# A gated-memory attention with two mixture layers: new numbers for the planner, q of block 0 turned from another queue, the router's fold in strips, a bound and a rounding on ScalarE

## The chip, the cores and the metric

The kernel runs on one core of a Trainium2 chip. The core has five engines with a queue each: TensorE (PE in the profile, PEld for its weight loads), VectorE (DVE), ScalarE (ACT), GpSimd (POOL) and SyncE (SP), which here only issues DMAs. Each works its queue in order. The metric is the time of one execution in microseconds; the median of three runs is given, lower is better.

## The reference, cut to what matters

```python
# attention: complex decay a per head and channel, only the real part of the state is read
scale = np.minimum(mag, 0.999) / (mag + 1e-06)          # mag = |a|
for t in range(S):                                      # S = 768, B = 4, H = 8, D = 48
    S_re, S_im = ar*S_re - ai*S_im + k[t] v[t]^T, ar*S_im + ai*S_re
    y[t] = q[t] @ S_re
x = (x @ w_a) * (x @ w_b) @ w_out                       # 3072 tokens, 384 -> 1536 -> 384
logits = x @ w_gate                                     # 8 experts
expert_idx = np.argmax(logits, axis=1)
out[mask] = gate_w[mask, None] * (np.maximum(x[mask] @ w1[e], 0.0) @ w2[e])
```

The attention is computed in chunks of 128 tokens. With the decay's logarithm summed along a chunk, q and k are multiplied by the magnitude (A or its inverse Bt) and by cosine and sine of the phase, and a masked product of both gives the same y. w_a, w_b and w_out arrive as 64-bit floats.

## The kernel before

There are 12 blocks of 256 tokens (two chunks each). For each block j the program has these parts:

- `loads` and `load_v` fetch re, im, q, k and v. `pre` computes on ACT, DVE and POOL the decay (`decay`, a scan), the tangent, the phase (`phase`, a scan), rounds the phase with MAGIC, takes cosine and sine, multiplies (`mul`) and turns the products with small DMAs into `kT` and `qT` (`turn`). For block 0 it is done in two halves of 128 tokens, which makes 12 turns for k and 12 for q, of 64 KB each.
- `attn` is the attention: scores `sc_p` (PE), `mask` to `sm` (DVE), k turned back `kn_p` (PE, copied by ACT), `y_p` (PE), then x as high and low part (`xH` on ACT, `xL` on DVE), and the state `kv_p` (PE), `T` (DVE).
- `planned_moe` is the first mixture: for each of 12 slices f, `up` writes `ab_p` (18 matmuls), ACT copies a half of it to g, DVE multiplies (`gate_b`), ACT makes gH, DVE or POOL gL, and `down` adds six products to `o`. Block 0 does it in plain fp32 with weights that were just unpacked (`up32`, `down32`, called the first gated products below); the later blocks do it with weights split into wH and wL (`parted`).
- `conv` loads one of 36 pieces of weights and unpacks it with three operations on DVE (L783, L786, L789: shift, low, sign). For each slice of w_out, PE also turns it (`wt_p`) and multiplies it with the router's weights (`wg_p`, the fold), with ACT copies between.
- Then the last block, and eight experts in a hand-merged order, from about 560 us on; the change doesn't touch this part.

Which engine's instruction stands where is not written by hand for the first 11 blocks. Each step is given to `Plan.add` with a cost, with what it reads and writes, and with a due time `at`; `Plan.run` simulates the five queues with these costs, takes the earliest step that is ready (on a tie that with the smaller due time), and then writes the instructions in that order. The chip follows this order on each queue, but not its times. PRE, ATT, CONV, M0, M1, SPLIT, SLOT, LOAD and AHEAD are the due times and paces; ON_POOL, GL_POOL and L_POOL say what goes to POOL instead of DVE. All the queues' DMAs stand on SP, except POOL's indirect ones.

Of the kernel before, what the change touches and what calls it, by code (L numbers as in the profile page):

```python
# [24 lines left out]
AHEAD = 14  # L25
LOAD = (4.0,2.0,7,30.0,2.0)
# [3 lines left out]
PRE = ((0.0, 20.0), (2.0, 22.0), (40.0, 70.0), (100.0, 125.0), (140.0, 166.0))  # L30
ATT = (26,66,110,156)
CONV = (22,1.8)
M0 = (40.0, 90.0)
M1 = 88
SPLIT = (84,1.2)
SLOT = 49.0
# [373 lines left out]
def fast(tc, q, k, v, a_re, a_im, w_a, w_b, w_out, w_gate, w1, w2, out, dram, x2d):  # L410

    nc = tc.nc
# [3 lines left out]
    with ExitStack() as mctx, ExitStack() as ctx:  # L416
# [18 lines left out]
        biases = const.tile([128, 4], F32, name="biases")  # L435
# [70 lines left out]
        def spans(i, src, nm, f, at):  # L506
# [13 lines left out]
            P.add("SP", 0.06, load, w=[("s", "bo"[i % 2], NF)], at=at, size=393, early=at)  # L520
# [235 lines left out]
        A32 = {}  # L756

        def conv(i, f, src, nm, at):
# [33 lines left out]
            P.add("SP", 0.06, load, r=[("bits", i - AHEAD)], w=[slot], at=start, early=start, size=393)  # L792
# [24 lines left out]
            t = P.add("PE", 0.28, turned, r=[slot], w=[("wt_p", f)], at=at + 2, take="sc")  # L817
            P.add("ACT", on("ACT", 384, True), kept, r=[("wt_p", f)], w=["rx"], at=at + 2, give=t)
            t = P.add("PE", 0.25, folded, r=["rx"], w=[("wg_p", f)], at=at + 3, take="sc")
# [115 lines left out]
        def planned_moe(j, lo, hi):  # L935
# [3 lines left out]
            def falls(f, at):  # L939
# [6 lines left out]
                for c in range(2):  # L946
                    P.add("ACT" if c == 0 else "DVE", on("DVE", DM) + 0.16, lambda c=c: close(j, c), r=[f"o{c}"] + ([("lgt", j % 2, 0)] if c else []), w=[("x2", c), ("lgt", j % 2, c)], at=at, alone=False)
                    P.add("SP", 0.06, lambda c=c: store(j, c), r=[("x2", c)], at=at, size=196)
# [30 lines left out]
        def load_v(j, c, at):  # L979
# [3 lines left out]
            P.add("SP", 0.06, go, w=[("v", (2 * j + c) % 3)], at=at, size=196)  # L983

        def loads(j, nms, at, parts=1):
# [17 lines left out]
            for i in range(2):  # L1003
                for nm in nms:
                    if parts == 1 and nm != "q":
                        if i == 0:
                            P.add("SP", 0.06, go(nm, 0, 2, True), w=[(nm, 0), (nm, 1)], at=at, size=393)
                    else:
                        made[nm, i] = \
                        P.add("SP", 0.06, go(nm, i, 1, i == 0), w=[(nm, 0), (nm, 1)] if i == 0 else [(nm, 1)], at=at + (4 if parts == 2 and i else 0), size=196, soft=made.get((nm, 0)))  # L1010

        def pre(j, lo, hi, t0, t1):
# [118 lines left out]
            add("DVE", lambda: nc.vector.tensor_scalar(out=T("Cc"), in0=T("F"), scalar1=MAGIC, scalar2=MAGIC, op0=ALU.add, op1=ALU.subtract), ks("F"), ks("Cc"), fast=True)  # L1131
            tt("frac", "F", "F", "Cc", ALU.subtract)
            add("DVE", lambda: nc.vector.tensor_copy(out=carry, in_=T("F")[:, :, n - 1, C - 1]), ks("F"), ["carry"], weight=0.16)
# [3 lines left out]
            act("F", "F", ACTF.Sin, scale=-TWO_PI)  # L1137

            def mul(src, c2, w):
                t = src if c2 else "Bt" if src == "k" else "A"  # L1140
                e, eng = pick(src + "01"[c2])

# [22 lines left out]
                for jj in range(3):  # L1165
                    first = c2 == 0 and lo == 0 and jj == 0
                    add("SP", turn(jj), ks(t) + [("column", t, lo)] + ([] if first else ks(src + "T")), (every(src + "T") if first else []) + [(src + "T", c, c2, jj) for c in cs], size=65 * n, key=src if first else None, soft=src)
# [5 lines left out]
            for i, (e, f, r, w, kw) in enumerate(todo):  # L1173
# [4 lines left out]
                if e == "SP":  # L1178
                    weight = 0.06
# [279 lines left out]
```

## Time and profile before

| | us |
|---|---|
| median of 3 runs (lowest, highest) | 935.42 (935.24, 936.86) |
| the profiled execution's own time | 934.75 |
| its span in the trace | 932.9 |
| PE busy | 865.6 (93%) |
| DVE busy | 606.7 (65%) |
| ACT busy | 446.6 (48%) |
| POOL busy | 288.5 (31%) |

The span runs from the first to the last instruction; 1.9 us lie around it. Busy shares are means over stages that differ: PE stands still for most of the first 41 us and is busy without a break for long stretches after. A busy PE is not PE at its peak.

### The profile page before, as it was taken

Reading aid. Unit: us, or ns where it says so; the run is one execution under the profiler, and the core shown is the slowest. Engines: PE = TensorE matmul, PEld = TensorE weight load, DVE = VectorE, ACT = ScalarE, POOL = GpSimd, SP = SyncE. Lnnn points to the kernel's source line nnn. Section 1 sums busy time; section 2 is a strip of 40 time slices with the busy share of each in tenths; the row PEclk is TensorE's granted clock in tenths of the full one; section 3 lists DMA queues with packets and bytes.
Section 4 is the critical chain, followed back from the end, with each engine's and each line's share of the span. In section 5 each row is a group of like instructions: output and inputs, shape, how many; then the busy total and the mean of one; then the engine's idle time right before and its main releaser. Section 6 shows DMA issues by size and latency. Waiting matters only on the chain. (4 is left out here: it accounts for less than half of the span.)

```text
span 932.9 us, 20023 instructions
## 1 busy us (share of the span) xinstructions
PE 865.6 (93%) x7948; PEld 829.9 (89%) x7948; DVE 606.7 (65%) x1261; ACT 446.6 (48%) x821; POOL 288.5 (31%) x285
## 2 busy tenths in 40 slices
PE   0399899899999999999999999999998999999993
PEld 0287789899999999999999999999997999999993
DVE  7799999968668678695858595325731644545440
ACT  6453567666656463645555552224531534434430
POOL 3100011143343334343434241213244451333311
PEclk9999999999999999999999999999998999999997
DMA  9394522540524643628172615024341543454601
GB/s 250 97 344 128 179 61 55 142 120 26 163 66 140 132 124 92 182 66 208 34 204 68 189 28 169 3 69 124 115 137 48 161 147 109 143 164 127 171 25 24
DMA packets 128900, 112.77 MB, mean 121 GB/s; under 512 B 36564, under 2 KB 123446, under 8 KB 128796
## 3 DMA queue, kind: packets, MB, share of 16 engines
q1 hardware_dynamic: 122620, 101.30, 38.0%
q0 software_dynamic: 6176, 10.08, 3.7%
q8 instruction: 65, 1.06, 0.5%
q14 instruction: 39, 0.32, 0.1%
HBM read 82.42 MB, written 10.56 MB: 100 GB/s over the span
## 5 line engine op out<-in xcount | busy, mean ns | idle before, releaser
L852 PE MATMUL ab_p<-xH,wa 128*128 128x256 f32 x792 | 168.4, 289 | 0.7 <-ACT xH L1259 0.7
L852 PE MATMUL ab_p<-xH,wb 128*128 128x256 f32 x792 | 162.6, 282 | 0.0
L880 POOL TENSOR_TENSOR gL<-g,gH 128x256 fp32r<-128x256 f32 x108 | 94.7, 877 | 213.0 <-ACT gH L876 204.9
L869 ACT COPY g<-ab_p 128x256 f32<-128x256 f32 x144 | 53.4, 371 | 181.8 <-PE ab_p L852 160.0
L889 PE MATMUL o<-wo,gH 128*128 128x392 f32 x528 | 139.7, 345 | 0.0
L852 PEld LDWEIGHTS ab_p<-xH,wa 128*128 128x128 f32 x792 | 131.3, 189 | 3.7 <-issue 1.9
L852 PEld LDWEIGHTS ab_p<-xH,wb 128*128 128x128 f32 x792 | 131.7, 190 | 0.0
L872 DVE TENSOR_TENSOR g<-g,ab_p 128x256 f32<-128x256 f32 x144 | 59.8, 415 | 99.8 <-ACT g L869 97.8
L852 PE MATMUL ab_p<-xL,wa 128*128 128x256 f32 x396 | 111.5, 282 | 1.8 <-DVE xL L1262 1.8
L852 PE MATMUL ab_p<-xL,wb 128*128 128x256 f32 x396 | 111.6, 282 | 0.0
L715 DVE SCALAR_TENSOR_TENSOR hL<-h_p,hH 128x256 fp32r<-128x256 f32 (+5 forms) x80 | 41.3, 517 | 97.2 <-ACT hH L714 85.5
L714 ACT ACTIVATE hH<-h_p 128x256 fp32r<-128x256 f32 (+5 forms) x80 | 36.6, 459 | 119.4 <-PE h_p L710 102.4
L889 PE MATMUL o<-wo,gL 128*128 128x392 f32 x264 | 90.1, 341 | 0.0
L889 PEld LDWEIGHTS o<-wo,gH 128*128 128x128 f32 x528 | 89.1, 189 | 0.7 <-issue 0.6
L710 PE MATMUL h_p<-sH,w1H 128*128 128x256 f32 (+5 forms) x240 | 78.3, 326 | 4.3 <-issue 4.0
L728 PE MATMUL o<-w2H,hH 128*128 128x384 f32 (+4 forms) x232 | 79.8, 344 | 0.0
L728 PE MATMUL o<-w2H,hL 128*128 128x384 f32 (+4 forms) x232 | 79.0, 341 | 0.0
L728 PE MATMUL o<-w2L,hH 128*128 128x384 f32 (+4 forms) x232 | 78.9, 340 | 0.0
L710 PE MATMUL h_p<-sH,w1L 128*128 128x256 f32 (+5 forms) x240 | 77.4, 323 | 0.0
L710 PE MATMUL h_p<-sL,w1H 128*128 128x256 f32 (+5 forms) x240 | 77.3, 322 | 0.0
L852 PEld LDWEIGHTS ab_p<-xL,wa 128*128 128x128 f32 x396 | 75.1, 190 | 2.4 <-DVE xL L1262 2.2
L876 ACT ACTIVATE gH<-g 128x256 fp32r<-128x256 f32 x132 | 54.6, 414 | 46.1 <-DVE g L872 45.2
(193 smaller groups left out, 1920.4 us busy)
## 6 DMA issues: line engine op xcount, KB each, us to landing
raw<-in_moe_w_dram SPq DMA_DIRECT2D x64, 384.0 KB
q<-in_q_dram SPq DMA_DIRECT2D x24, 192.0 KB
v<-in_v_dram SPq DMA_DIRECT2D x24, 192.0 KB
raw<-in_moe_w_a_dram SPq DMA_DIRECT2D x12, 384.0 KB
raw<-in_moe_w_b_dram SPq DMA_DIRECT2D x12, 384.0 KB
raw<-in_moe_w_out_dram SPq DMA_DIRECT2D x12, 384.0 KB
x2d<-x SPq DMA_DIRECT2D x24, 192.0 KB
ck<-in_moe_w_a_dram SPq DMA_DIRECT2D x12, 384.0 KB
```

The costliest lines, as they stand in the source:

```text
L710: nc.tensor.matmul(out=t, lhsT=lh[:, o:o + 128], rhs=rh[:, kk].rearrange("p c t -> p (c t)"), start=n == 0, stop=n == 8)
L714: nc.scalar.activation(out=hH, in_=t, func=ACTF.Relu)
L715: nc.vector.scalar_tensor_tensor(out=hL, in0=t, scalar=0.0, in1=hH.bitcast(F32), op0=ALU.max, op1=ALU.subtract)
L728: nc.tensor.matmul(out=G["o", c], lhsT=lh[:, c * r:(c + 1) * r], rhs=rh, start=f == 0 and n == 0, stop=f == NH - 1 and n == 2)
L852: nc.tensor.matmul(out=t[:, i], lhsT=lh[:, kk * 128:(kk + 1) * 128], rhs=rh[:, kk], start=n == 0, stop=n == 8)
L869: nc.scalar.copy(out=G["g", j, f], in_=G["ab", j, f][:, 0])
L872: nc.vector.tensor_tensor(out=G["g", j, f], in0=G["g", j, f], in1=G["ab", j, f][:, 1], op=ALU.mult)
L876: nc.scalar.activation(out=G["H", j, f], in_=G["g", j, f], func=ACTF.Copy)
L880: eng.tensor_tensor(out=G["L", j, f], in0=G["g", j, f], in1=G["H", j, f].bitcast(F32), op=ALU.subtract)
L889: nc.tensor.matmul(out=G["o", j, c], lhsT=lh[:, c * C:(c + 1) * C], rhs=rh, start=f == first and n == 0, stop=f == last and n == 2)
```

## The change

Seven edits:

1. The planner's table of due times and paces is another, and so are ON_POOL, GL_POOL and L_POOL: of block 0, POOL takes two products with the magnitudes (kA), two with the cosine (k0) and the squares, DVE the sums and products that POOL had; from block 3 on POOL has six of a block's products (add, sub, k0, k1, q0, q1) instead of three; of block 2's first mixture gL is made on DVE; six of the 36 wL are made on POOL.
2. The planner counts 0.5 (0.55 for turns) for each DMA that SP issues, instead of 0.06, and other costs for three PE steps.
3. The 12 turns of q in block 0 are issued by ACT instead of SP (`BY_ACT`).
4. The fold is done in four strips of 32 output rows: 12 matmuls for each of the 12 slices instead of 3.
5. The bound of the decay's logarithm was a DVE operation; it is now the Relu of an ACT activation, with the sign turned and the constant added in the next Exp.
6. Rounding with MAGIC was a DVE operation with two constants; now ACT adds MAGIC and one DVE operation takes off both MAGIC and the phase (so with the sign turned, which the sine's scale gives back).
7. The tiles of the weights are named once at the start, which sets the places they get; no instruction hangs on it.

```diff
-AHEAD = 14
-LOAD = (4.0,2.0,7,30.0,2.0)
+AHEAD = 18
+LOAD = (2.94, 2.02, 6, 26.92, 2.0)
...
-ATT = (26,66,110,156)
+ATT = (26, 69.6, 99.2, 153.5)
...
-    0: ("sq", "add", "imul", "k1", "q1"),
-    1: ("x",),
-    2: ("qA", "q1"),
-    3: ("add", "qA", "q1"),
+    0: ('k0', 'kA', 'sq'),
+    1: ('add',),
+    2: ('qA',),
+    3: ('add', 'frac', 'k0', 'k1', 'q0', 'q1', 'sub'),
 }
-GL_POOL = (2, 12)
-L_POOL = ()
+BY_ACT = (0,)
+GL_POOL = (3, 12)
+L_POOL = (0, 6, 12, 18, 24, 30)
...
-                    nc.tensor.matmul(out=K["t"], lhsT=K["wt"][:, kk], rhs=wg[:, kk], start=kk == 0, stop=kk == 2)
+                    for s in range(0, 128, 32):
+                        nc.tensor.matmul(out=K["t"][s:s + 32], lhsT=K["wt"][:, kk, s:s + 32], rhs=wg[:, kk], start=kk == 0, stop=kk == 2)
...
-            add("DVE", lambda: nc.vector.tensor_scalar(out=T("A"), in0=T("A"), scalar1=0.5, scalar2=math.log(0.999), op0=ALU.mult, op1=ALU.min), ks("A"), ks("A"), fast=True)
+            act("A", "A", ACTF.Relu, scale=-0.5, bias=biases[:, 4:5])
...
-            tt("sub", "A", "A", "Bt", ALU.subtract)
-            act("A", "A", ACTF.Exp)
+            tt("sub", "A", "A", "Bt", ALU.add)
+            act("A", "A", ACTF.Exp, scale=-1.0, bias=biases[:, 4:5])
...
-            add("DVE", lambda: nc.vector.tensor_scalar(out=T("Cc"), in0=T("F"), scalar1=MAGIC, scalar2=MAGIC, op0=ALU.add, op1=ALU.subtract), ks("F"), ks("Cc"), fast=True)
-            tt("frac", "F", "F", "Cc", ALU.subtract)
+            add("ACT", lambda: nc.scalar.activation(out=T("Cc"), in_=T("F"), func=ACTF.Copy, bias=MAGIC), ks("F"), ks("Cc"))
+            add("DVE", lambda: nc.vector.scalar_tensor_tensor(out=T("F"), in0=T("Cc"), scalar=MAGIC, in1=T("F"), op0=ALU.subtract, op1=ALU.subtract), ks("F", "Cc"), ks("F"))
...
+                by = ("ACT", nc.scalar) if j in BY_ACT and src == "q" else ("SP", nc.sync)
...
-                        nc.sync.dma_start(out=pq[src, j][c2 * 3 + jj::6, :, lo:hi], in_=full()[:, jj, :, 0:w])
+                        by[1].dma_start(out=pq[src, j][c2 * 3 + jj::6, :, lo:hi], in_=full()[:, jj, :, 0:w])
...
-                if e == "SP":
-                    weight = 0.06
+                if "size" in kw:
+                    weight = 0.55
```

How the order moves is shown at three places. Line numbers of the change are 6 to 8 higher than those of before.

**ACT, block 0, second half.** X holds the phase, then cosine and sine; wt and raw are the copies for the turned slice and for the fold, for which PE waits and which wait for PE. Before, ACT's queue reads:

```order
L1134 ACTIVATE X<-X 128x3x128
L1046 ACTIVATE X<-X,biases 128x3x128
L1046 ACTIVATE X<-X 128x3x128
L1055 ACT_TABLE_LOAD
L807 COPY wt<-wt_p 128x384
L815 COPY raw<-wg_p 128x8
L830 ACTIVATE wo_318<-raw 128x392
```

In the change the turns of q stand between them, the first three ahead of the second half's phase and the later ones around the copies for the first fold:

```order
L1138 ACTIVATE X<-X 128x3x128
L1166 DMA qT<-A 16x8x129 x3
L1141 ACTIVATE X<-X 128x3x128
L1053 ACTIVATE X<-X,biases 128x3x128
L1053 ACTIVATE X<-X 128x3x128
L1062 ACT_TABLE_LOAD
L1166 DMA qT<-A 16x8x129 x2
L1166 DMA qT<-q 16x8x129
L1166 DMA qT<-A 16x8x129
L813 COPY wt<-wt_p 128x384
L1166 DMA qT<-q 16x8x129
L822 COPY raw<-wg_p 128x8
```

Right behind these rows ACT has the third qT<-q of the first chunk, then an operation of block 1 and the three of the second chunk. SP keeps the 12 turns of k. So 21 issues, 12 on SP and 9 on ACT, stand ahead of or at the last that the first chunk needs.

**DVE, the masks of block 0.** sm is the masked score of four heads; each chunk has two. ca and raw are unpacking, X and A block 1's preparation. Before, four rows and then four more lie between the two masks of the first chunk and those of the second:

```order
L1213 TENSOR_TENSOR sm<-sc_p,causal 128x512 x2
L1050 TENSOR_TENSOR Bt<-A,Bt 128x768
L836 TENSOR_TENSOR wa_252<-raw,wa_252 128x384
L783 TENSOR_SCALAR ca<-raw 128x384
L1080 SCALAR_TENSOR_TENSOR X,seen<-X,re 128x768
L1213 TENSOR_TENSOR sm<-sc_p,causal 128x512
L786 SCALAR_TENSOR_TENSOR ca<-raw,ca 128x384
L1274 SCALAR_TENSOR_TENSOR T_133<-kv_p,qT 96x8x48
L789 SCALAR_TENSOR_TENSOR raw<-raw,ca 128x384
L783 TENSOR_SCALAR ca<-raw 128x384
L1213 TENSOR_TENSOR sm<-sc_p,causal 128x512
```

In the change the second chunk's masks stand behind 20 rows; these are the last ones:

```order
L792 SCALAR_TENSOR_TENSOR ca<-raw,ca 128x384
L1057 TENSOR_TENSOR A<-A,Bt 128x6x128
L795 SCALAR_TENSOR_TENSOR raw<-raw,ca 128x384
L789 TENSOR_SCALAR ca<-raw 128x384
L1106 TENSOR_REDUCE seen<-X 128x1
L1221 TENSOR_TENSOR sm<-sc_p,causal 128x512 x2
```

The 20 rows are 5 of L789 (shift), 8 of L792 and L795 (low and sign), one T, and six operations on 768 elements of block 1. What stood behind the masks before, up to block 1's product A<-A,Bt, now stands ahead of them.

**PE, the end of block 1's attention.** ab_p<-x,raw is a half of a slice of block 0's mixture, ab_p<-xH,wa the first matmul of block 1's, which needs xH and xL. Before, from the state on:

```order
L1268 MATMUL kv_p<-v_130,kn 32x48 x24
L803 MATMUL wt_p<-ident,raw 128x128 x3
L852 MATMUL ab_p<-xH,wa_252 128x256
L852 MATMUL ab_p<-xL,wa_252 128x256
L852 MATMUL ab_p<-xH,wa_252 128x256 x2
```

In the change:

```order
L1256 MATMUL y_p<-qT,T_170 32x128 x4
L809 MATMUL wt_p<-ident,raw 128x128 x3
L1276 MATMUL kv_p<-v_167,kn 32x48 x24
L866 MATMUL ab_p<-x,raw 128x256 x6
L819 MATMUL wg_p<-wg,wt 32x8 x12
L809 MATMUL wt_p<-ident,raw 128x128 x3
L872 MATMUL o_716<-raw,g 128x392
L872 MATMUL o_718<-raw,g 128x392
L819 MATMUL wg_p<-wg,wt 32x8 x12
L859 MATMUL ab_p<-xH,wa_290 128x256
```

A slice of block 0, two folds and a `down32` now stand between y and the matmuls that need xH and xL. At the end of block 2's attention twelve products of `down` stand there in the same way (before, five small matmuls of the router), and ten slices of block 0 stand ahead of block 1's attention instead of eleven.

## Rows read from the trace of the kernel before

**Rows 1.** Busy time by stage: stretch, us, PE, PEld, DVE, ACT, POOL (count), PEclk, DMA

```profile
56.95:109.70 52.75, 50.99 (x244) 41.55 (x243) 51.57 (x116) 22.77 (x46) 0.00 (x0) 1.00 0.71 224
109.70:124.69 14.99, 12.05 (x277) 10.85 (x275) 14.14 (x30) 13.84 (x26) 0.00 (x0) 1.00 0.08 17
...
166.37:183.71 17.34, 14.52 (x253) 13.23 (x252) 17.00 (x43) 11.40 (x18) 2.34 (x2) 1.00 0.55 157
183.71:210.00 26.29, 25.75 (x190) 25.45 (x191) 19.02 (x27) 15.91 (x28) 12.07 (x11) 0.94 0.39 110
210.00:560.00 350.00, 350.00 (x3957) 340.17 (x3958) 260.87 (x540) 193.41 (x347) 136.77 (x122) 1.00 0.43 115
```

**Rows 2.** PE in order of time: start, us, instruction, idle before it

```profile
41.37 3.78 PE L1209 MATMUL sc_p<-qT,kT 96*128 96x128 f32 x16 [4.92 <-DMA qT<-q]
...
56.95 2.76 PE L859 MATMUL ab_p<-x,raw 128*128 128x256 f32 x12
```

**Rows 3.** SP's queue in order of time

```profile
27.64 1.93 SPq L1158 DMA_DIRECT2D kT<-Bt  x3
...
39.27 0.60 SPq L1158 DMA_DIRECT2D qT<-q  x1
```

**Rows 4.** ACT in order of time

```profile
29.65 0.52 ACT L1134 ACTIVATE X<-X 128x384 f32<-128x384 f32 x1 [3.08 <-DVE X L1050]
...
31.30 1.28 ACT L1055 ACT_TABLE_LOAD   x1
34.47 0.48 ACT L807 COPY wt<-wt_p 128x384 f32<-128x384 f32 x1 [1.89 <-PE wt_p L803]
```

**Rows 5.** DVE in order of time

```profile
45.19 0.69 DVE L1213 TENSOR_TENSOR sm<-sc_p,causal 128x512 f32<-128x512 f32 x1 [1.01 <-PE sc_p L1209]
...
52.29 0.69 DVE L1213 TENSOR_TENSOR sm<-sc_p,causal 128x512 f32<-128x512 f32 x1 [0.74 <-PE sc_p L1209]
...
58.18 0.35 DVE L783 TENSOR_SCALAR ca<-raw 128x384 uint32<-128x384 uint32 x1
58.45 0.95 DVE L1050 TENSOR_TENSOR A<-A,Bt 128x768 f32<-128x768 f32 x1
59.31 0.55 DVE L786 SCALAR_TENSOR_TENSOR ca<-raw,ca 128x384 uint32<-128x384 uint32 x1
59.78 0.35 DVE L783 TENSOR_SCALAR ca<-raw 128x384 uint32<-128x384 uint32 x1
...
112.92 0.69 DVE L1213 TENSOR_TENSOR sm<-sc_p,causal 128x512 f32<-128x512 f32 x1
```

**Rows 6.** PE in order of time: the state's strips, a fold, what follows each

```profile
55.70 0.86 PE L1268 MATMUL kv_p<-v,kn 128*32 128x48 f32 x48
56.49 0.62 PE L803 MATMUL wt_p<-ident,raw 128*128 128x128 f32 x3
...
59.55 0.73 PE L812 MATMUL wg_p<-wg,wt 128*128 128x8 f32 x6
60.14 2.84 PE L859 MATMUL ab_p<-x,raw 128*128 128x256 f32 x12
```

**Rows 7.** PE in order of time: a down, an up, the next down

```profile
140.21 0.52 PE L889 MATMUL o<-wo,gH 128*128 128x392 f32 x2
...
141.28 0.28 PE L852 MATMUL ab_p<-xH,wa 128*128 128x256 f32 x1
...
143.40 0.52 PE L889 MATMUL o<-wo,gH 128*128 128x392 f32 x2
```

**Rows 8.** The page's costliest groups: busy us, mean ns of one, idle before

```profile
L880 POOL TENSOR_TENSOR gL<-g,gH 128x256 fp32r<-128x256 f32 x108 | 94.7, 877 | 213.0 <-ACT gH L876 204.9
...
L872 DVE TENSOR_TENSOR g<-g,ab_p 128x256 f32<-128x256 f32 x144 | 59.8, 415 | 99.8 <-ACT g L869 97.8
...
L876 ACT ACTIVATE gH<-g 128x256 fp32r<-128x256 f32 x132 | 54.6, 414 | 46.1 <-DVE g L872 45.2
```

**Rows 9.** POOL's groups from 210 to 560 us, as in Rows 8

```profile
L1147 POOL TENSOR_TENSOR q<-q,X 128x768 f32<-128x768 f32 x8 | 15.2, 1903 | 15.0 <-DVE A L1147 15.0
```

More of the change, by code (lines that the diff above doesn't have):

```diff
@@ L518, in reduce @@
                 return lambda: nc.vector.tensor_reduce(out=span[:, n, i:i + 1], in_=G["r"][:, :, 1].bitcast(F32), axis=AX.X, op=op, apply_absolute_value=True)
[L520 removed]
+            P.add("SP", 0.5, load, w=[("s", "bo"[i % 2], NF)], at=at, size=393, early=at)
             for n, op in enumerate((ALU.max, ALU.min)):
@@ L756, in fast @@
         A32 = {}
+        for nms in ("ab", "o"):
+            for f in range(NF):
+                for nm in nms:
+                    wts.tile([128, 2, 384 + (NE if nm == "o" else 0)], F32R, tag=f"w{nm}{f}", name=f"w{nm}{f}")
         def conv(i, f, src, nm, at):
@@ L790, in sign @@
                 unpacked[i] = getattr(r, "ins", r).name
-            P.add("SP", 0.06, load, r=[("bits", i - AHEAD)], w=[slot], at=start, early=start, size=393)
+            P.add("SP", 0.5, load, r=[("bits", i - AHEAD)], w=[slot], at=start, early=start, size=393)
             P.add("DVE", on("DVE", 384, fast=True), shift, r=[slot], w=[ca], at=at)
@@ L811, in folded @@
                 for kk in range(3):
-                    nc.tensor.matmul(out=K["t"], lhsT=K["wt"][:, kk], rhs=wg[:, kk], start=kk == 0, stop=kk == 2)
+                    for s in range(0, 128, 32):
+                        nc.tensor.matmul(out=K["t"][s:s + 32], lhsT=K["wt"][:, kk, s:s + 32], rhs=wg[:, kk], start=kk == 0, stop=kk == 2)
             def beside():
                 nc.scalar.copy(out=A32[nm, f][:, DM:DM + NE], in_=K["t"])
-            t = P.add("PE", 0.28, turned, r=[slot], w=[("wt_p", f)], at=at + 2, take="sc")
+            t = P.add("PE", 0.34, turned, r=[slot], w=[("wt_p", f)], at=at + 2, take="sc")
             P.add("ACT", on("ACT", 384, True), kept, r=[("wt_p", f)], w=["rx"], at=at + 2, give=t)
-            t = P.add("PE", 0.25, folded, r=["rx"], w=[("wg_p", f)], at=at + 3, take="sc")
+            t = P.add("PE", 0.41, folded, r=["rx"], w=[("wg_p", f)], at=at + 3, take="sc")
             P.add("ACT", 0.17, beside, r=[("wg_p", f)], w=[("A32", nm, f)], at=at + 3, give=t)
@@ L1006, in loads @@
                         if i == 0:
-                            P.add("SP", 0.06, go(nm, 0, 2, True), w=[(nm, 0), (nm, 1)], at=at, size=393)
+                            P.add("SP", 0.5, go(nm, 0, 2, True), w=[(nm, 0), (nm, 1)], at=at, size=393)
                     else:
                         made[nm, i] = \
-                        P.add("SP", 0.06, go(nm, i, 1, i == 0), w=[(nm, 0), (nm, 1)] if i == 0 else [(nm, 1)], at=at + (4 if parts == 2 and i else 0), size=196, soft=made.get((nm, 0)))
+                        P.add("SP", 0.5, go(nm, i, 1, i == 0), w=[(nm, 0), (nm, 1)] if i == 0 else [(nm, 1)], at=at + (4 if parts == 2 and i else 0), size=196, soft=made.get((nm, 0)))
         def pre(j, lo, hi, t0, t1):
@@ L1166, in mul @@
                     first = c2 == 0 and lo == 0 and jj == 0
-                    add("SP", turn(jj), ks(t) + [("column", t, lo)] + ([] if first else ks(src + "T")), (every(src + "T") if first else []) + [(src + "T", c, c2, jj) for c in cs], size=65 * n, key=src if first else None, soft=src)
+                    add(by[0], turn(jj), ks(t) + [("column", t, lo)] + ([] if first else ks(src + "T")), (every(src + "T") if first else []) + [(src + "T", c, c2, jj) for c in cs], size=65 * n, key=src if first else None, soft=src)
             mul("k", 0, C)
@@ L1301, in attn @@
                 if not last:
-                    add("PE", 1.36, kv, [("kn", 0), ("kn", 1), v_], [("kv_p", j, c)], take="sc")
+                    add("PE", 0.82, kv, [("kn", 0), ("kn", 1), v_], [("kv_p", j, c)], take="sc")
                     add("DVE", on("DVE", 384), sum_, [("kv_p", j, c), T_] + qk, [To_], give=True, alone=False)
```

25 lines of the change are left out of this document (13 added, 12 removed).

## The prediction

> **What bounds the kernel now.** I read the busy time by stage first, with stages cut where PE's work changes. From 210 to 560 us PE is busy for all of 350.00 us at full granted clock [rows 1]: nothing there can be gained but by less PE work. Before, PE's idle time is the difference of two numbers in a row: 1.76 us of 52.75 while block 0's mixture runs, 2.94 of 14.99 in block 1's attention, 2.82 of 17.34 in block 2's, 0.54 of 26.29 behind it, where the mean granted clock is 0.94, which is 6% of 26.29, or 1.6 us at the full level [rows 1]. Together 9.7 us can come from there. Ahead of all this stands the start: PE in order of time shows the first gated product at 56.95, behind an attention that began at 41.37 when the last qT landed [rows 2]. In the same stages DVE is full: 51.57 of 52.75, 14.14 of 14.99 and 17.00 of 17.34 [rows 1]. So up to 184 us PE is paced by what ACT, DVE and the turns deliver, and from there on by itself. A microsecond won by 184 us reaches the end; a cheaper DVE behind that is worth nothing.
>
> **The start.** In SP's queue 12 turns of k and 12 of q follow each other from 27.64, each about 0.62 (three in 1.93) [rows 3]; the last q of the first chunk is issued at 39.27 and scores start at 41.37, so landing takes 1.5 after the issue's 0.60 [rows 2, 3]. The changed preparation loses a DVE step for the bound and one for the rounding and gets its sums from DVE instead of POOL; I put the first turn of k at 26.5, about 1 earlier. On ACT, from some 26.9 on: three issues of q at 0.6 are 1.8; then absolute value, cosine, sine and table load, which before went from 29.65 to 32.58, so 2.9 [rows 4]; four issues, 2.4; the copy wt 0.48 [rows 4], an issue 0.6, the small copy 0.2, an issue 0.6; and 0.8 as an estimate for the two waits for PE. That makes 36.7, and with landing 38.2 instead of 41.37. No issue on ACT's queue is in the trace, so its cost is taken from SP's; below 0.6 the wait for PE's fold keeps the date, above it nine issues carry it on.
>
> But the masks eat this. From the start of the scores to the second mask's end went 4.5 before (45.19 and 0.69) [rows 2, 5]; so DVE is free at 42.7. Now 20 rows come ahead of the second chunk's masks: 5 shifts of 0.27, 8 low and sign operations and the T at 0.47, six operations on 768 elements of 0.86 at most, less 0.4 for the bound's faster form. The spacing of starts gives these figures (58.18, 58.45, 59.31, 59.78) [rows 5]. That is 1.4, 4.2 and 4.8, together 10.4, so masks from 53.2 to 54.5 against 52.29 to 53.0 before. From the first of these to the first gated product went 4.7 before (56.95 less 52.29), with y, the copy of x and the state; the pair of masks is now together, so y starts a mask earlier. I get 57.5: **0.5 later**, though scores start 3 earlier. What DVE did in that time is not lost; it is three pieces of weights and most of block 1's preparation further.
>
> **The fold.** Six rows, a fold, take from 59.55 to 60.14, 0.59. No fold of strips is in the trace; the state's matmuls are strips of 32 outputs, and 48 rows take from 55.70 to 56.49, 16.5 ns each [rows 6]. The 24 rows of a new fold would then take 0.40; each gives 0.19, and nine folds behind the start give **1.7**. If strips do not overlap, a row costs 0.098 as now and a fold 2.4; that is the other bound, and a rival. I take the strips' row, since it is the same shape but for the number of columns. The Trainium skill, TensorEngine Tiling (Array Packing), section Tiling Modes, Key Properties, speaks against the edit: a change of the tiling mode drains TensorE, and this is two changes a fold. The trace has such a change where the state's strips end and a full-width wt_p begins at 56.49, with no gap that the row shows; by the row the fold gains, by the rule some of it goes back, and the page has no figure for the drain.
>
> **The waits of PE.** DVE's rows from these masks to the masks of block 1's attention are 93: 53 of unpacking, 13 splits, 10 gates, 9 operations on 768 elements, 9 scans. With the spacings above, 0.42 for a gate [rows 8] and, as an estimate, 0.5 for a piece of a scan, they sum to 45, so DVE is there at about 99.5; before, it began that mask at 112.92 [rows 5], after PE's scores had begun at 109.70 [rows 1]. PE has in that time ten slices instead of eleven; ten elevenths of 52.75, less 1.7, make 46.3, so it comes at about 104. DVE waits for PE now, not PE for DVE. Of block 0's 1.76 I leave 0.5 (each turned slice now has other work between it and its fold, which hides ACT's copy): **1.3**. Of block 1's 2.94 I leave 0.8, since masks find DVE free and a slice covers xL: **2.1**. Of block 2's 2.82 I leave 1.0: twelve products, 2 × 1.07 by the spacing of a down [rows 7], cover xH and xL: **1.8**. The clock falls there after PE has stood still in three waits, and with these filled I leave 0.4 of 1.6: **1.2**. Of 0.54, 0.3 stays: **0.2**.
>
> Costed at nothing: the bound and the rounding on ACT in later blocks, and gL of block 2 on DVE (12 × 0.33 in a stage where DVE has 7 us free) [rows 1]; ACT's cover is the 157 us it stands idle from 210 to 560. The named tiles move no instruction. Fewer DVE operations behind 210 are covered by a full PE.
>
> **The sum.** Against the profiled execution's 934.75: + 0.5 − 1.7 − 1.3 − 2.1 − 1.8 − 1.2 − 0.2 = − 7.8, so 926.95. That execution lies 0.67 under the median of the runs, so I predict 927.6.
>
> **Rivals.** *The two queues' issues take turns.* Then 21 issues at 0.62 from 26.5 end at 39.5, scores start at 41.0, 2.8 later than above, and all behind it: 930.4. For it: three issues in a row never overlap on SP; against it: that is one queue. The Trainium skill says so too: DMA: Bandwidth & Descriptors, Issuing engines are not separate DMA queues, grants the second queue only the sequencer's time, and Perfetto Trace Analysis says that the descriptor generator is locked for exclusive use. By these pages this rival would stand at 930.4 as well; no run has two queues yet.
>
> *The waits stay.* The planner's order leans on its own costs; if ACT or DVE is late at each attention as before, only the start and the folds remain: − 1.2, so 934.2. For it: an order in which 20 rows stand ahead of two masks. Against it: DVE's 4 us in hand.
>
> *GpSimd becomes the one that PE waits for; slower.* A down follows its slice by an up, a down and an up: 2.12 + 1.07 + 2.12 = 5.3 [rows 7]. The way to gL is a copy, the gate, gH and gL, 0.4 + 0.42 + 0.41 + 0.88 = 2.1 [rows 8], which leaves 3.2. From block 3 on, two products of 768 often stand together on POOL; at 1.90 each [rows 9] they hold a gL up for 3.8, 0.6 too long, and POOL's next product can take the same again. At 1.5 us in each of eight stages it is 12 us, 939.6; it decides from 1.0 a stage. Against it: idle time of POOL before gL is 213.0 us [rows 8].
>
> *Strips do not overlap; slower.* A fold at 2.4 costs 1.8 more than now, nine of them 16; instead of the gain of 1.7 that is 945.5. It decides from 1.3 us a fold. Against it: the state's 48 rows.
>
> **How the numbers follow.** Forecast 0.58 (923 to 932 by its own: the start 3 earlier if the second masks find DVE ahead of my count, 4 later if ACT's issues cost 1.0), turns 0.20, waits 0.09, GpSimd 0.08, strips 0.05. The range 922 to 935 holds the first three, but for the forecast's edges. A measurement tells 0.2%, 1.9 us, from no change. Faster by more than that, under 933.5: forecast, turns and a part of GpSimd's smaller prices, 0.81. Within: mostly the waits, 0.08. Slower: 0.11.
>
> **What would show it.** Right: issues of qT on ACT's queue of about 0.6; scores at about 38, the second chunk's masks at 53, the first gated product between 56 and 59; 24 rows of a fold in 0.4 to 0.5; PE idle in the two attentions 1 us or less each, block 2's scores near 162 instead of 166.37 [rows 1]; full clock behind it; no PE wait for gL. Wrong: issues on ACT over 1 us; a first gated product behind 60; idle PE between 210 and 560.

## The result: faster, by more than forecast

| | before | changed |
|---|---|---|
| median of the runs beside each other (lowest, highest) | 935.73 (935.24, 936.86), 4 runs | 924.37 (922.71, 927.3), 4 runs |
| ratio, 95% interval | | 0.9882 [0.9862, 0.9901] |
| the profiled execution's own time, its span | 934.75, 932.9 | 922.71, 920.9 |
| PE, DVE, ACT, POOL busy | 865.6, 606.7, 446.6, 288.5 | 858.1, 570.8, 463.2, 321.5 |

927.6 was forecast with 922 to 935. The sum of the working was −7.8 against the profiled execution; −12.0 came between the two profiled ones. The change's is the fastest of its four executions; by the medians it is −11.4.

### The profile after

Busy time by stage of the changed kernel, columns as in [rows 1]: block 0's mixture, block 1's attention, block 2's attention up to its first product, the rest up to block 3's scores, and a long stretch behind.

```profile
58.98:102.92 43.94, 43.65 (x324) 33.85 (x319) 41.38 (x91) 22.23 (x44) 1.02 (x1) 1.00 0.64 202
102.92:119.29 16.37, 16.37 (x343) 14.23 (x342) 16.06 (x35) 11.38 (x23) 1.02 (x1) 1.00 0.33 75
159.77:176.96 17.19, 17.19 (x273) 16.30 (x272) 15.90 (x34) 11.82 (x19) 2.20 (x2) 1.00 0.49 133
176.96:199.57 22.61, 21.14 (x169) 20.79 (x167) 16.88 (x34) 14.40 (x27) 11.46 (x7) 1.00 0.35 94
246.71:590.47 343.76, 343.76 (x3806) 333.11 (x3805) 219.69 (x487) 187.54 (x340) 157.34 (x147) 1.00 0.43 116
```

PE stands still for 0.29 us in block 0's mixture and not at all in the two attentions. A new wait of 1.47 stands ahead of block 3's scores. PE in order of time shows it, and the start:

```profile
38.96 3.75 PE L1217 MATMUL sc_p<-qT,kT 96*128 96x128 f32 x16
...
49.77 0.60 PE L809 MATMUL wt_p<-ident,raw 128*128 128x128 f32 x3 [1.92 <-issue]
50.94 0.38 PE L819 MATMUL wg_p<-wg,wt 128*32 128x8 f32 x24 [0.57 <-ACT wt L813]
51.37 3.44 PE L1217 MATMUL sc_p<-qT,kT 96*128 96x128 f32 x16
...
55.92 0.55 PE L1226 MATMUL kn_p<-ident,kT 96*128 96x96 f32 x4 [0.57 <-ACT kn L1231]
56.41 0.43 PE L1256 MATMUL y_p<-sm,v 128*32 128x128 f32 x8
...
58.98 1.35 PE L866 MATMUL ab_p<-x,raw 128*128 128x256 f32 x5
...
102.92 1.95 PE L1217 MATMUL sc_p<-qT,kT 96*128 96x128 f32 x16
...
199.57 2.02 PE L1217 MATMUL sc_p<-qT,kT 96*128 96x128 f32 x16 [1.47 <-DMA qT<-q]
```

Scores start at 38.96 (41.37 in [rows 2]), but the first gated product at 58.98, 2.0 later. The second chunk's scores wait behind a turned slice and take 3.44 us, where the same 16 rows take 1.95 at 102.92.

DVE in order of time: the wait for the first chunk's state, the second chunk's masks and the row ahead of them, and the first mask of block 1:

```profile
47.91 0.55 DVE L1282 SCALAR_TENSOR_TENSOR T<-kv_p,qT 96x384 f32<-96x384 f32 x1 [1.01 <-PE kv_p L1276]
...
54.21 0.94 DVE L1106 TENSOR_REDUCE seen<-X 128x1 f32<-128x768 f32 x1
55.07 1.27 DVE L1221 TENSOR_TENSOR sm<-sc_p,causal 128x512 f32<-128x512 f32 x2
...
104.03 0.68 DVE L1221 TENSOR_TENSOR sm<-sc_p,causal 128x512 f32<-128x512 f32 x1
```

From 47.91 to the masks at 55.07 DVE has no gap. Block 1's first mask begins 1.11 behind the start of its scores; before, it was 3.22 (112.92 and 109.70).

The two queues that issue turns in the start, SP and then ACT with its DMA issues:

```profile
32.25 1.97 SPq L1166 DMA_DIRECT2D kT<-Bt  x3
34.26 1.90 SPq L1166 DMA_DIRECT2D kT<-k  x3
```

```profile
31.21 1.28 ACT L1062 ACT_TABLE_LOAD   x1
31.41 1.20 ACTq L1166 DMA_DIRECT2D qT<-A  x2
32.65 0.61 ACTq L1166 DMA_DIRECT2D qT<-q  x1
33.30 0.62 ACTq L1166 DMA_DIRECT2D qT<-A  x1
```

From 32.25 to 34.22 SP issues three turns and ACT two, each in about 0.6; two more issues lie under ACT's table load.

To compare times at equal work, a row is needed ahead of which PE has done the same in both kernels. By the order, as many products of each kind stand ahead of the second chunk's scores in block 4, and again in block 11. PE in order of time, before and then changed:

```profile
256.33 1.05 PE L1209 MATMUL sc_p<-qT,kT 96*128 96x128 f32 x8
...
602.33 1.14 PE L1209 MATMUL sc_p<-qT,kT 96*128 96x128 f32 x8
```

```profile
246.71 1.06 PE L1217 MATMUL sc_p<-qT,kT 96*128 96x128 f32 x8
...
590.47 1.14 PE L1217 MATMUL sc_p<-qT,kT 96*128 96x128 f32 x8
```

9.62 us are won by block 4 and 11.86 by block 11. The 2.24 between come from a stretch in which PE is busy all the time at full granted clock in both kernels: 346.00 against 343.76.

### The profile page after: what moved, and what is told of

The parts are those of the page before. It is cut to its first block, busy times and chain, and to the rows that moved or that the text cites. A ratio compares the mean times of both kernels' runs of the same rounds, so it can differ in the third digit from the quotient of the medians.

```text
span 920.9 us, 20515 instructions
## 1 busy us (share of the span) xinstructions
PE 858.1 (93%) x8164; PEld 820.6 (89%) x8164; DVE 570.8 (62%) x1219; ACT 463.2 (50%) x847; POOL 321.5 (35%) x302
## 5 line engine op out<-in xcount | busy, mean ns | idle before, releaser
L859 PE MATMUL ab_p<-xH,wa 128*128 128x256 f32 x792 | 166.4, 287 | 0.0
L859 PE MATMUL ab_p<-xH,wb 128*128 128x256 f32 x792 | 159.7, 279 | 0.0
L887 POOL TENSOR_TENSOR gL<-g,gH 128x256 fp32r<-128x256 f32 x96 | 78.2, 816 | 174.6 <-ACT gH L883 173.9
```

Of the source, the lines that this page charges most:

```text
L859: nc.tensor.matmul(out=t[:, i], lhsT=lh[:, kk * 128:(kk + 1) * 128], rhs=rh[:, kk], start=n == 0, stop=n == 8)
L887: eng.tensor_tensor(out=G["L", j, f], in0=G["g", j, f], in1=G["H", j, f].bitcast(F32), op=ALU.subtract)
```

## The experiments

All times beside before's runs on the same chip, whose medians were 934.7 to 935.7. The dates are those of the profiled execution of each: first gated product, the two rows of equal work, the end of the span.

| kernel | median (runs) | ratio, 95% interval | gated | block 4 | block 11 | end |
|---|---|---|---|---|---|---|
| before | 935.73 (4) | | 56.95 | 256.33 | 602.33 | 932.9 |
| changed | 924.37 (4) | 0.9882 [0.9862, 0.9901] | 58.98 | 246.71 | 590.47 | 920.9 |
| changed_again | 923.26 (6) | 0.9892 [0.9865, 0.9919] | 60.70 | 248.68 | 592.55 | 921.1 |
| full_fold | 929.62 (6) | 0.9940 [0.9922, 0.9959] | 64.95 | 258.40 | 602.16 | 932.0 |
| q_on_sp | 928.27 (10) | 0.9921 [0.9896, 0.9946] | 63.53 | 251.54 | 595.36 | 925.8 |
| before_strips | 930.17 (4) | 0.9948 [0.9931, 0.9965] | 56.00 | 251.26 | 597.53 | 925.5 |
| unnamed | 927.43 (10) | 0.9931 [0.9909, 0.9952] | 61.68 | 250.08 | 595.54 | 924.9 |
| old_table | 930.79 (4) | 0.9954 [0.9938, 0.9971] | 60.46 | 252.54 | 598.12 | 930.4 |
| new_table | 933.89 (10) | 0.9989 [0.9974, 1.0004] | 53.51 | 252.25 | 601.04 | 931.6 |
| dve_bound | 928.0 (10) | 0.9930 [0.9904, 0.9956] | 60.83 | 251.25 | 595.20 | 926.6 |
| old_pools | 928.98 (7) | 0.9932 [0.9908, 0.9957] | 67.77 | 252.18 | 596.98 | 930.2 |
| c1_early | 922.27 (4) | 0.9866 [0.9850, 0.9883] | 54.90 | 246.40 | 590.16 | 918.2 |
| b3_dve | 926.62 (4) | 0.9913 [0.9896, 0.9929] | 60.56 | 248.91 | 592.82 | 923.3 |
| early_q3 | 923.02 (6) | 0.9882 [0.9859, 0.9906] | 54.34 | 245.74 | 589.54 | 918.6 |

From block 11's row to the end the same work takes 328.0 (before_strips, c1_early) to 333.2 us (old_pools), though no edit is there. So a single time tells 2 us badly, and the dates at equal work tell more. A profiled execution can also lie some us from its kernel's median: full_fold's took 933.74, old_pools' 931.90, before_strips' 927.31, c1_early's 919.87 and early_q3's 920.41.

### changed_again: the scatter

> The changed kernel itself once more, beside the next two on the same chip, since its executions scatter over 4.6 us (922.7 to 927.3) and those of before over 1.6. If the scatter comes from TensorE's speed in block 0's second chunk, the profiled execution shows either fast rows there (a y of 16 products in 0.40 us, first gated product near 59) and a time near 923, or slow ones (0.65 us, near 61.6) and a time near 926. Median expected 924.5.

PE in the second chunk, and the granted clock there (columns as in [rows 1]):

```profile
50.57 3.78 PE L1217 MATMUL sc_p<-qT,kT 96*128 96x128 f32 x16
...
56.40 0.66 PE L1256 MATMUL y_p<-sm,v 128*32 128x128 f32 x8
...
60.70 8.04 PE L866 MATMUL ab_p<-x,raw 128*128 128x256 f32 x36
```

```profile
50.00:60.00 10.00, 9.29 (x121) 8.48 (x124) 8.38 (x19) 2.88 (x6) 0.00 (x0) 0.50 1.03 342
```

These are the slow rows, at the level of 1.2 GHz (0.50), after PE had stood still for 2.5 us in two pieces just ahead. In the first profiled execution the column falls to 0.50 as well, after the same two pieces, but is at 1.00 again when y begins at 56.41. The first gated product is 1.72 later than in the other execution of the same kernel, and block 11's row 2.08. Yet the time was 922.79, not 926: the end took 328.55 instead of 330.43. The slow rows are real; the scatter of the times isn't explained by them alone. Another source of it shows in the next run.

### full_fold and before_strips: the fold

```diff
-                    for s in range(0, 128, 32):
-                        nc.tensor.matmul(out=K["t"][s:s + 32], lhsT=K["wt"][:, kk, s:s + 32], rhs=wg[:, kk], start=kk == 0, stop=kk == 2)
+                    nc.tensor.matmul(out=K["t"], lhsT=K["wt"][:, kk], rhs=wg[:, kk], start=kk == 0, stop=kk == 2)
```

before_strips is the same the other way round, in the kernel before.

> The changed kernel with the fold as it was (3 full-width products for each of 12 folds), the planner's costs and so every queue's order unchanged. Theory, a fold behind the first gated product is on PE's path and its strips save 0.30 us (spacing 0.31 against 0.59 to 0.62): nine of them give 2.7, and the three ahead of it move the first gated product by 0.3 at most; about 3 us slower than the changed kernel. Rival, DVE paces the stage, so that a longer fold only fills PE's waits: 0.5 us slower or less.

> The kernel before with the fold in strips and nothing else; its planner's costs and every queue's order are unchanged. Theory, folds are on PE's path there as well: ten folds behind the first gated product at 0.3 each, 3 us faster. Rival, DVE paces that stage (51.57 busy of 52.75), so what PE saves turns into waiting for DVE ahead of block 1's scores and masks: 0.5 us or less.

A slice, its fold and what follows, PE in order of time, the changed kernel and then full_fold:

```profile
72.56 2.76 PE L866 MATMUL ab_p<-x,raw 128*128 128x256 f32 x12
75.25 0.38 PE L819 MATMUL wg_p<-wg,wt 128*32 128x8 f32 x24
75.56 1.65 PE L872 MATMUL o<-raw,g 128*128 128x392 f32 x4
```

```profile
78.53 2.76 PE L865 MATMUL ab_p<-x,raw 128*128 128x256 f32 x12
81.13 0.73 PE L818 MATMUL wg_p<-wg,wt 128*128 128x8 f32 x6
81.72 1.63 PE L871 MATMUL o<-raw,g 128*128 128x392 f32 x4
```

The fold itself takes 0.31 against 0.59. But the slice ahead of it takes 2.69 when strips follow and 2.60 when they don't. From the slice's start to the next product it is 3.00 against 3.19: a fold gives 0.19, not the 0.30 that I expected of these runs. From the first gated product to block 1's scores full_fold takes 45.01 and the changed kernel 43.94; six folds lie there, 0.18 each.

The larger part lies ahead, where the same rows run slowly. full_fold there:

```profile
46.98 1.45 PE L818 MATMUL wg_p<-wg,wt 128*128 128x8 f32 x6
48.36 1.50 PE L1275 MATMUL kv_p<-v,kn 128*32 128x48 f32 x48
...
53.23 1.45 PE L818 MATMUL wg_p<-wg,wt 128*128 128x8 f32 x6 [0.57 <-ACT wt L813]
54.54 3.76 PE L1216 MATMUL sc_p<-qT,kT 96*128 96x128 f32 x16
```

The folds at 46.98 and 53.23 take until 48.36 and 54.54, 1.38 and 1.31, where strips take 0.35 and 0.43. full_fold's second scores start at 54.54, 3.97 later than changed_again's, and block 2's scores at 167.39, 5.89 later (161.50).

Of its 9.72 us by block 4 the rest is for the most part not the fold's price. PE in order of time at block 3's scores, and the granted clock from there:

```profile
208.37 3.75 PE L1216 MATMUL sc_p<-qT,kT 96*128 96x128 f32 x16 [2.69 <-DMA qT<-q]
```

```profile
208.00:214.00 6.00, 5.63 (x27) 5.66 (x28) 4.72 (x8) 4.03 (x8) 2.43 (x1) 0.50 0.68 209
```

SP's fill among block 3's turns took 1.93 us to issue in this execution (0.59 in the changed kernel), PE waited 2.69 for the turns (1.30 in changed_again), and then the clock fell to its lower level: from block 3's first scores to its second went 7.77 us instead of 4.71. No other profiled execution of the change's order shows that there. It is one of two long ones of full_fold (933.74 and 934.09; the other four took 928.89 to 929.64); whether the long executions of the other kernels have the same hole is not shown.

In before_strips the stage from the first gated product to block 1's scores takes 51.26 instead of 52.75, and the first gated product comes 0.95 earlier. That is half of its 5.07 by block 4; most of the rest is the clock behind block 2's attention, and 0.5 the wait at block 3's scores, which is not there in this execution, the fastest of four. From 180 to 190 us, before_strips and then before:

```profile
180.00:190.00 10.00, 9.08 (x74) 9.01 (x74) 8.55 (x19) 5.24 (x11) 3.66 (x4) 1.00 0.14 37
```

```profile
180.00:190.00 10.00, 7.82 (x75) 7.26 (x67) 8.46 (x21) 5.02 (x8) 3.61 (x4) 0.83 0.28 80
```

before_strips has the same waits around there (0.64, 0.55, 0.71 and 0.92 between 176 and 181), and the clock did not fall. Of the two theories neither holds alone: folds are on PE's path, but at 0.19 each behind the first gated product, and in the changed kernel they count for more ahead of it.

### q_on_sp and c1_early: is the start what counts?

```diff
-                by = ("ACT", nc.scalar) if j in BY_ACT and src == "q" else ("SP", nc.sync)
+                by = ("ACT", nc.sync) if j in BY_ACT and src == "q" else ("SP", nc.sync)
```

c1_early moves the steps of block 0's second chunk and first mixture (`pull`) up to 7 us ahead in the finished order, x being a step's place in it and y the new one:

```diff
+EARLY = (7.0, 50.8, 96.0)
...
+        key = {}
         for x, n, _ in out:
+            y = x - EARLY[0] * (1 - (x - EARLY[1]) / (EARLY[2] - EARLY[1])) if n in self.pull and EARLY[1] <= x < EARLY[2] else x
+            key[n] = max([y] + [key[m] for m in ops[n]["need"]])
+        for _, _, n in sorted((key[n], i, n) for i, (_, n, _) in enumerate(out)):
```

> The changed kernel with q of block 0 issued by SyncE again at the places that the planner gave it on ScalarE; the order of PE, DVE and POOL is unchanged. SyncE then issues 21 turns and 4 loads of weights by the last that the first chunk needs, about 15 us from 26.7, so scores start at about 43 instead of 38.96. Theory, the start is a chain that all behind it follows: the first gated product comes 2.5 to 4 later and the kernel is about 3 us slower. Rival, the start is slack (DVE has 20 rows to do ahead of the second chunk's masks in either case): under 0.7 us.

> The changed kernel with block 0's second chunk and first mixture up to 7 us earlier in every queue (less and less until 96 us), all else in the planner's order. The second chunk's scores then stand ahead of the third turned slice. Theory, the start sets the end: PE has no hole of 3 us ahead of the second scores, its rows there run at full speed (16 score rows in 2.0 us instead of 3.4), the first gated product comes at about 53 instead of 59 and the kernel is 4 us faster than the changed one, about 920.5. Rival, DVE paces PE until block 1's masks: what the start wins comes back as PE waiting for unpacked weights and gates ahead of block 1's scores, which gain at most 1.5.

With q on SP scores start at 41.88. Against changed_again, which has the same slow rows, the first gated product is 2.83 later, block 4's row 2.86 and block 11's 2.81: all of it reaches the end. With the second chunk early the first gated product is 4.08 earlier than in the changed kernel, and block 4's row only 0.31. PE in order of time, the three longest waits that c1_early has in between:

```profile
81.08 1.14 PE L876 MATMUL ab_p<-x,raw 128*128 128x256 f32 x4 [0.96 <-DVE raw L803]
...
100.05 1.65 PE L882 MATMUL o<-raw,g 128*128 128x392 f32 x4 [1.24 <-ACT raw L830]
...
199.02 1.24 PE L1227 MATMUL sc_p<-qT,kT 96*128 96x128 f32 x9 [1.73 <-DMA qT<-q]
```

It waits for unpacked weights, for a fold and for block 3's turns. The changed kernel has 0.29 of the second and 1.47 of the third too, so 2.2 us of these are new, and 0.5 come in two smaller waits. By block 1's scores (101.54) 1.38 of the 4.08 are left, as the rival had it.

The two differ in DVE. From 38 to 46 us DVE is busy for 1.03 us in q_on_sp and 5.01 in the changed kernel: a later first chunk holds DVE up, whose order has its masks there. An earlier second chunk takes no work off DVE. So the first gated product's date alone is not the term; as far as these two runs show, it is the date up to block 3 at which DVE gets its work done.

### unnamed: the places of the weights

```diff
-        for nms in ("ab", "o"):
-            for f in range(NF):
-                for nm in nms:
-                    wts.tile([128, 2, 384 + (NE if nm == "o" else 0)], F32R, tag=f"w{nm}{f}", name=f"w{nm}{f}")
```

> The changed kernel without the tiles of the weights named at the start: the weights get other places in SBUF, every queue's order is unchanged. From 250 to 590 us, where PE has no wait in either kernel, the changed kernel's equal work (from block 4's second scores to block 11's second scores) takes 243.8... no wait between them: 343.76 against 346.00 us. Theory, the places of the weights make that: this kernel takes 346 there and is 2.2 us slower than the changed one. Rival, it is the order of the rows or the other engines' load: 343.8 there and no change.

Between the two rows of equal work, unnamed and then full_fold, which has the named tiles:

```profile
250.08:595.54 345.46, 345.46 (x3806) 334.82 (x3805) 219.27 (x487) 187.86 (x339) 156.59 (x147) 1.00 0.42 115
```

```profile
258.40:602.16 343.76, 343.76 (x3805) 333.08 (x3805) 219.93 (x487) 187.83 (x339) 157.04 (x147) 1.00 0.43 116
```

Every kernel with the change's order and named tiles takes 343.76 to 343.95 there (changed, changed_again, full_fold, q_on_sp, dve_bound, b3_dve, c1_early, early_q3); without the names it is 345.46, with the same order and the same load of DVE, ACT and POOL. So 1.7 of the 2.24 come from where the weights lie. By which property of the places, the runs don't show. The order has a part in it: with the named tiles but the order of before (old_table) PE is busy for 345.02 in that stretch, against 346.00 before, and with the GpSimd sets of before (old_pools) for 344.80.

### old_table and new_table: numbers or operations

old_table is the changed kernel with the planner's numbers, costs and GpSimd sets of before; new_table is the kernel before with those of the change:

```diff
-AHEAD = 14
-LOAD = (4.0,2.0,7,30.0,2.0)
+AHEAD = 18
+LOAD = (2.94, 2.02, 6, 26.92, 2.0)
...
-            P.add("SP", 0.06, load, r=[("bits", i - AHEAD)], w=[slot], at=start, early=start, size=393)
+            P.add("SP", 0.5, load, r=[("bits", i - AHEAD)], w=[slot], at=start, early=start, size=393)
```

> The changed kernel's operations (strips, bound and rounding on ScalarE, q of block 0 from ScalarE's queue, named tiles) with the planner's numbers, costs and GpSimd sets of before. Theory, the operations give strips (2.7), the weights' places (1.7) and some of the start (1), and the waits of PE in the attentions of blocks 1 and 2 stay, 4 to 6 us of them, since the order makes those: about 930. Rival, DVE's saved operations fill the waits by themselves: about 925, as the changed kernel.

> The kernel before with the planner's numbers, costs and GpSimd sets of the change, and none of its operations. Theory, the order alone fills PE's waits in the two attentions: idle there 1 us or less in all, and 4 to 6 us faster than before, about 930. Rival, these numbers are only good with the cheaper operations: DVE, which has two operations a block more and turns of q on SyncE, is late again, waits stay, within 2 us of before.

Both theories were half right. The operations alone give 4.7. PE's waits in block 2's attention stay (y 1.10 for masks, 0.72 for xH, 0.91 for xL), but those in block 1's are gone. The numbers alone give 1.6, with an interval that holds 1: PE has no wait left in the two attentions and new_table is 4.08 ahead by block 4, but only 1.29 by block 11, for its masks come late again at 485 and 535 us:

```profile
PE kn_p L1218 <- DVE sm L1213: 2.3, 2, 1.4
```

4.7 and 1.6 are 6.3; together they give 11.4. Some 5 us are had only when operations and order come together. Which of the operations the order needs, these two runs don't tell; the bound and the rounding alone are tried next.

### dve_bound and old_pools: DVE's relief

```diff
-            act("A", "A", ACTF.Relu, scale=-0.5, bias=biases[:, 4:5])
+            add("ACT", lambda: nc.vector.tensor_scalar(out=T("A"), in0=T("A"), scalar1=0.5, scalar2=math.log(0.999), op0=ALU.mult, op1=ALU.min), ks("A"), ks("A"), bias=True)
...
-            add("ACT", lambda: nc.scalar.activation(out=T("Cc"), in_=T("F"), func=ACTF.Copy, bias=MAGIC), ks("F"), ks("Cc"))
+            add("ACT", lambda: nc.vector.tensor_scalar(out=T("Cc"), in0=T("F"), scalar1=MAGIC, scalar2=MAGIC, op0=ALU.add, op1=ALU.subtract), ks("F"), ks("Cc"))
```

> The changed kernel with the bound and the rounding on DVE again (two more operations of 0.55 us a block there, two fewer on ScalarE), at the places in the order that the planner gave them on ScalarE. Theory, DVE's saved operations are part of why the masks come in time: the new numbers without the new operations left PE waits for sm at 216, 485 and 535 us, so such waits appear here and the kernel is 2 to 4 us slower. Rival, as I costed it, they are worth nothing behind 210 us (DVE stands idle a quarter of the time there): under 1 us.

Against changed_again: first gated product 0.13 later, block 4's row 2.57, block 11's 2.65. So two operations of DVE a block cost 2.4 us between 61 and 250 and nothing behind (343.95); the waits at 485 and 535 that the theory named don't come. Part of it is no gap in PE's rows at all; the weight loads show it:

```profile
157.93 0.19 PEld L859 LDWEIGHTS ab_p<-xH,wb 128*128 128x128 f32 x1 [0.30 <-ACT wb L837]
158.53 0.30 PEld L859 LDWEIGHTS ab_p<-xH,wb 128*128 128x128 f32 x2 [0.29 <-DVE wb L843]
```

The last splits of block 1's weights are late by two rows there, where PE's own rows count as busy.

old_pools takes ON_POOL, GL_POOL and L_POOL of before:

```diff
-    0: ('k0', 'kA', 'sq'),
-    1: ('add',),
-    2: ('qA',),
-    3: ('add', 'frac', 'k0', 'k1', 'q0', 'q1', 'sub'),
+    0: ("sq", "add", "imul", "k1", "q1"),
+    1: ("x",),
+    2: ("qA", "q1"),
+    3: ("add", "qA", "q1"),
...
-GL_POOL = (3, 12)
-L_POOL = (0, 6, 12, 18, 24, 30)
+GL_POOL = (2, 12)
+L_POOL = ()
```

> The changed kernel with the GpSimd sets of before (block 0's sums and products, block 2's gL, three products a block behind instead of six, no wL), its other numbers and costs unchanged; the planner makes a new order from them. Theory, the new sets are part of what fills PE's waits, since DVE is full up to 184 us: waits for masks, unpacked weights or xL come back in the attentions, 2 to 4 us at equal work by block 4's second scores. Rival, the sets only move work where PE is full anyway (from 210 on): under 1 us there, and the same end within 1.5.

The size was right (3.5 by block 4 against changed_again), the place wrong: no wait came back in the attentions. The planner put block 0's first gated product at 67.77, 7.1 later, and PE then waited for nothing until 204. As far as this run shows, the sets buy DVE time, and the planner's order decides whether that becomes an earlier start or fewer waits.

### b3_dve and early_q3: the new wait

GpSimd makes block 3's four products one behind the other, and DVE has a gL to make meanwhile. POOL and DVE in order of time, changed kernel:

```profile
186.85 1.86 POOL L1155 TENSOR_TENSOR Bt<-k,X 128x768 f32<-128x768 f32 x1
188.66 1.75 POOL L1155 TENSOR_TENSOR A<-q,X 128x768 f32<-128x768 f32 x1
190.36 1.84 POOL L1155 TENSOR_TENSOR k<-k,X 128x768 f32<-128x768 f32 x1
192.16 1.73 POOL L1155 TENSOR_TENSOR q<-q,X 128x768 f32<-128x768 f32 x1
```

```profile
189.37 4.81 DVE L887 TENSOR_TENSOR gL<-g,gH 128x256 fp32r<-128x256 f32 x1
```

b3_dve gives the two products with the sine to DVE; early_q3 is c1_early with block 3's turns of q issued by ACT:

```diff
+                if j == 3 and c2:
+                    eng = nc.vector
```

```diff
-                by = ("ACT", nc.scalar) if j in BY_ACT and src == "q" else ("SP", nc.sync)
+                by = ("ACT", nc.scalar) if j in BY_ACT and src == "q" else ("SP", nc.scalar if j == 3 and src == "q" else nc.sync)
```

> The changed kernel with block 3's two products with the sine on DVE instead of GpSimd, all orders else the same. In the changed kernel GpSimd makes block 3's four products one behind the other (186.85 to 193.9), a gL of DVE takes 4.81 us meanwhile, the turns of q are issued until 197.1, and PE waits 1.47 us for them at 199.57. Theory, GpSimd's chain is what PE waits for there: the wait goes, 1.5 us faster, and the executions scatter less, since a wait there can cost the clock as well. Rival, the wait moves to DVE, which has two more products of 0.95 to do between gates: no gain.

> The early second chunk (as in c1_early), and block 3's six turns of q issued by ScalarE instead of SyncE, order else the same. With block 3's products on DVE the wait of 1.4 us at its scores stayed, and SyncE then issued 12 turns and a fill back to back from 190.9 to 199.3. Theory, SyncE's 13 issues of 0.62 behind the first product are what PE waits for: with six of them on ScalarE the wait falls under 0.4 us, what the start won is kept, and the kernel is 1.5 us faster than c1_early, about 920.5. Rival, ScalarE's queue stands behind GpSimd's last product (193.9), copies and gates come late and PE waits for those instead: no gain, about 922.3.

On DVE the last product is done 5.6 us behind the start of the first (189.00 to 194.59), on GpSimd it was 7.0 (186.85 to 193.89); yet the wait is 1.37. The first theory falls: SP has 12 turns and a fill to issue behind the first product, back to back from 190.88 to 199.26 in b3_dve, and in as many us, 8.4, in the changed kernel. With six of them on ACT the wait is 0.26. But block 4's row is only 0.66 earlier than in c1_early, for masks that PE had not waited for are now late by 0.61 and 0.40. The early versions end 2 to 3 us ahead of the changed kernel in their profiles, and by medians (922.27 and 923.02 against 924.37 and 923.26) no version is faster beyond doubt.

## Why the prediction was right, and what it missed

**The mechanism held, with nothing to spare.** PE's waits fill: 1.76, 2.94 and 2.82 us [rows 1] became 0.29, 0 and 0. I had left 0.5, 0.8 and 1.0, so these terms gave 7.2 instead of 5.2. Blocks 1 and 2 had their scores at 102.92 and 159.77, near the 104 and 162 of the working. But DVE came to block 1's masks at 104.03, not at 99.5: its 93 rows since the masks of block 0 took 49.0 us instead of 45. DVE was just in time, and the 4 us in hand that I held against *The waits stay* were not there.

**The fold** gave the 0.19 that I forecast, by another sum: 0.40 was put for 24 strips, and they take 0.31 and 0.09 for the change of the tiling. The Trainium skill, TensorEngine Tiling (Array Packing), section Tiling Modes, Key Properties, says that a change of mode drains TensorE; the rows agree, with 0.09 more between the start of the row ahead and the first strip (2.69 against 2.60). What I missed are the three folds ahead of the first gated product, where PE's rows are slow: a full-width one costs 0.9 to 1.0 more than strips there.

**The start** was mis-sized: + 0.5 stood there, + 2.0 was measured, and + 3.75 in the second execution. Masks came at 55.07 instead of 53.2, for two reasons: the scores had begun 0.76 later than forecast, and the T among the 20 rows waited 1.01 for the first chunk's state, a wait that I had put at nothing. But the step that failed is the one from masks to the first gated product. I let y follow the masks; it follows PE's own chain. In changed_again the masks came 0.79 earlier (54.28) and y began at 56.40, as at 56.41 here, right behind `kn_p`, which stands behind the second chunk's scores. These stood behind a slice to be turned, ahead of which PE was idle for 1.92 and 0.57, and took 3.44 us instead of 1.95: here a hole in PE's work cost its length and then the clock. c1_early, with the scores ahead of that slice, has y at 52.03, 8 rows in 0.43, and the first gated product at 54.90.

**The clock** behind block 2's attention is at 1.00 as forecast, but my reason isn't shown: before_strips stands still in the same waits and keeps 1.00.

**0.54 at block 3's scores** I put at 0.3; it is 1.47. By b3_dve and early_q3 it is SP's queue that PE waits for there: 12 turns and a fill, issued behind GpSimd's first product.

**Costed at nothing, wrongly.** "The named tiles move no instruction" was true, and yet they are worth 1.7 us: with the same rows in the same order PE takes longer without them. The bound and the rounding are worth nothing behind 250, as I said, but 2.4 us ahead of it, where DVE has no cover: I argued with ACT's idle time from 210 on and forgot the first four blocks.

**The sum.** By measured terms: + 2.03 − 1.7 − 1.47 − 2.94 − 2.82 − 1.6 + 0.93 = − 7.6, and 1.7 for the places makes 9.3 of 12.0. 2.8 stay without a place of their own: about 2 ahead of block 4's row, where waits can hide in weight loads as in dve_bound, 0.5 in the long stretch and 0.2 in the end. That the measured terms come so near to − 7.8 is luck: the start and block 3's scores cost 2.7 more than forecast, and the filled waits and the clock gave 2.4 more. Nor do the terms simply add: old_table and new_table have − 4.7 and − 1.6 alone, − 11.4 together. The other way round, to take one part away (strips, q from ACT, names, bound and rounding, GpSimd sets) costs 3.1 to 5.3 us by the medians, some 20 for the five.

**The rivals.** *The two queues take turns* falls: five turns in 2 us on two queues, each at its 0.6. *The waits stay* falls for the whole change; for the operations alone it holds in block 2, and for the numbers alone the waits come later, at masks behind 210 us. *GpSimd becomes waited for*: PE never waits for its gL; of its chain of products at block 3 only the first sets a date, that at which SP begins with the turns. *Strips don't overlap* falls.

## What to carry to other kernels

Where one engine paces another, an order and a saving on the pacing engine are not two gains that add up: measure both halves alone and together, at rows of equal work and not at the end. A chunk that is only a few microseconds late can cost twice: here TensorE's rows ran at half the speed after holes of 2.5 us (block 0's second chunk) and 2.69 us (block 3's scores in full_fold). Where the pacing engine isn't helped, an earlier start comes back as waits.

## What the hardware showed that I had not expected

- The places of the weights in SBUF alone change the time of a stretch in which PE never waits: 345.46 against 343.76 us for the same rows in the same order.
- Issues on ACT's queue run beside those on SP's and under ACT's own table load. The Trainium skill, DMA: Bandwidth & Descriptors, section Issuing engines are not separate DMA queues, grants just this, the sequencer's time; so it speaks against issues in turn, beside which the prediction had put it. Here that time was worth 2.8 us (q_on_sp against changed_again).
- A gL of 0.42 on DVE took 4.81, from 189.37 to 194.18, and ended 0.29 behind the last of the products of GpSimd that lay across it (192.16 and 1.73). The Trainium skill, SBUF — State Buffer, section Who interferes with whom, calls the port that the two share an exclusive lock; the row agrees, and shows that DVE can lose it to several products in a row. The gL at 196.35 met only one (196.09 to 197.84): it took 1.77 and ended 0.28 behind that.
- The column of the granted clock read 1.00 where the first chunk's 16 score rows took 3.75 us, twice what they take later; in full_fold it read 1.00 from 60 to 64 where 8 rows of y took 0.65 instead of 0.40. There the rows' own length tells more than the column.
